# Memory attention with routed experts: one load of the gate weights, sums by two products, stores over two queues, a new order

## The chip, the cores and the metric

The kernel runs on one core of a Trainium2 chip. The metric is device time in microseconds (us), median of the timed runs. Engines are called PE (TensorE; PEld are its weight loads), DVE (VectorE), ACT (ScalarE), POOL (GpSimd) and SP (SyncE, which here issues loads and stores).

## What is computed

The reference has two parts. Attention over 32 memories for each of 8 batches and 8 heads (576 rows, 64 columns), then a mixture of 8 experts in which each of the 4608 rows goes to one expert.

```python
a = softmax(phi)                                  # 8 x 8 x 576 x 32, sums with 1e-9
k_m, v_m = a^T k, a^T v                           # per head: 32 memories x 64
attn = softmax(q k_m^T / 8)                       # 576 x 32
x = (attn v_m), heads side by side                # 4608 x 512
expert = argmax(x w_gate); gate = its probability # w_gate 512 x 8
out[row] = gate * relu(x w1[expert]) w2[expert]   # w1 512 x 1024, w2 1024 x 512
```

## The kernel before

Each batch b (0 to 7) is assumed to go to one expert: its guess is the most frequent expert of the batch (for batch 0 a guess from sums of the values). Rows that belong elsewhere ("strays") are listed in DRAM and done in slots of 64 rows at the end; of the last batch's rows, those that a stray slot wrote are added back from a DRAM buffer `late`. [...]

A batch has two parts. `front` makes the weights of the memories (steps A to C), the memory step E, which multiplies them with k and v (kvm), their sums D and scaling F, transposed keys G and G1, scores J, softmax K to M3 in a transposed layout, the high and low halves S and T of the attention weights, logits R, and the expert index by rank products X3, histogram R4 and index R6. LW loads w1 of that expert (four quarters), D0 to D3 load w2, W0 to W3 split it into halves. U0 and U1 multiply the memories' values with w1 (so that the experts' first layer works on 64 memories per head group), UH and UL split the result. `experts` makes the dense products: i00 to i17 (two halves of the rows, 8 column blocks, 6 products each), relu and split e, output products o (o00 to o33 in four row tiles of four parts with 6 products each, o40 to o43 for the tail of 64 rows with 4), evacuation y0 to y4, z for the tail, and stores.

The work of all engines follows one list, ORDER, written out by hand: "3X4" is step X4 of batch 3, "30J" step 0J (head group 0) of batch 3. `plan` calls the steps in that order, and each engine (PE, DVE, ACT, POOL, SP) keeps the order of its own instructions, so that a step waits for whatever stands ahead of it on its engine. Constants made before the list are free to move. Buffers: PSUM tag "mm" has 4 that are used in turn (pu of U0 and U1, ph, py), w1 and w2 share 6 raw buffers, output tiles y have 2, so that y of one tile waits until the stores of the tile two before have landed. At the start the PE does products on ones (`keep_warm`).

Lines that matter below: w_gate is loaded by three small loads on POOL's queue, twice in one layout (L172, for both halves of the partitions) and once in another (L173), copied in `constants_late` (L185). The sums of the memories' weights come in E, at the end, by products with `sel` (L304), a 64x32 tile for each head and half:

```python
for c in range(C + 1):
    ...
    nc.tensor.matmul(kvm[s][o0:o0 + 32, 2 * D:], lhsT=sel[s0, :], rhs=zp[s0, g, j:j + 1], start=True, stop=True)
```

and D adds 1e-9 (L310, two instructions) and takes the reciprocal (L311). `store` (L682) issues a tile's stores of 32 rows on SP; for the last tail of the last batch on ACT.

Of the kernel before, what the change touches and what calls it, by code (L numbers as in the profile page):

```python
# [27 lines left out]
0i11 0W1 0e15 0e10 1E 0i14 1D 0W2 10F 10Q 11Q 2L0 11F 0i13 0R3 1V 1V1 10G 0X 11G 1V2 0e14 1V3 1G1 0e11 0o00 0W3 10J
0X3 10K1 10K 0o01 0R4 0CE 0e13 10K2 10K3 11J 11K 0i16 11K1 0o10 0X1 11K2 0e16 11K3 10L 10M 20A 0o02 0o30 11L 10M0 10M1
0o03 10M2 2L1 0o11 0X4 11M 11M0 20A1 11M1 10M3 11M2 2LQ 0y0 0o31 0i17 11M3 21A 1R 1R1 1S1 1R2 1R3 0o12 0e17 0o40 1X3  # L30
0o32 0o33 1R4 0o13 11N 1R6 1X 1LW 0y3 0o41 1X4 0o42 0y1 21A1 1S0 1D3 0o20 2A2 10N 0o21 20Q 1D1 0o43 0o22 0o23 21B 1T0
20B 0X2 0X5 21Q 20C 21C 1U0 0y4 0y2 1T1 1UH10 0z 1U1 0X6 1UL10 1UH01 1UH00 1UL01 2E 1UL00 1D0 1i00 1UH11 1i01 1i02 00N
# [35 lines left out]
7i13 7i07 7o00 7entries 7load21 7load13 7W2 7W3 7e04 7e13 7gather 7e07 7load20 7o01 7i11 7load10 7load11 7o02 7o03
# [15 lines left out]
def kernel(  # L84
# [16 lines left out]
    P = 128  # L101
# [546 lines left out]
    def experts(b, st):  # L648
# [30 lines left out]
        def row(i, t):  # L679
            return (4 * i + t) // (T // 2), (4 * i + t) % (T // 2)  # L680
# [461 lines left out]
```

## Time and profile before

| | us |
|---|---|
| median of 3 timed runs | 432.77 (432.46 to 433.3) |
| profiled execution, device time | 436.48 |
| its span, first to last instruction | 434.7 |
| PE busy | 418.5 |
| DVE, ACT, POOL busy | 270.5, 192.8, 190.2 |

The profile comes from one execution, whose own time is 436.48 us. Busy times of engines overlap; the ends of products are modelled, so that a PE that is called busy may still stand between two starts. The rows on which the prediction rests stand in a section of their own.

### The profile page before, as it was taken

Reading aid. Unit: us, or ns where it says so; the run is one execution under the profiler, and the core shown is the slowest. Engines: PE = TensorE matmul, PEld = TensorE weight load, DVE = VectorE, ACT = ScalarE, POOL = GpSimd, SP = SyncE. Lnnn points to the kernel's source line nnn. Section 1 sums busy time; section 2 is a strip of 40 time slices with the busy share of each in tenths; the row PEclk is TensorE's granted clock in tenths of the full one; section 3 lists DMA queues with packets and bytes.
Section 4 is the critical chain, followed back from the end, with each engine's and each line's share of the span. In section 5 each row is a group of like instructions: output and inputs, shape, how many; then the busy total and the mean of one; then the engine's idle time right before and its main releaser. Section 6 shows DMA issues by size and latency. Waiting matters only on the chain.

```text
span 434.7 us, 11303 instructions
## 1 busy us (share of the span) xinstructions
PE 418.5 (96%) x4339; PEld 327.3 (75%) x4339; DVE 270.5 (62%) x690; ACT 192.8 (44%) x515; POOL 190.2 (44%) x270
## 2 busy tenths in 40 slices
PE   8879999899999999999999999999999999999992
PEld 4539787578867888688877887778869877698871
DVE  5478777386654777467645767569646756546422
ACT  3158424463345624463526434554247521745610
POOL 4565641047135453167044442366305866663530
PEclk9999999999999999999999999999999999999997
DMA  8898885790697817593277825694186007776302
GB/s 256 311 398 328 285 336 181 244 344 8 168 331 231 314 53 237 171 362 142 77 271 255 307 78 147 230 341 157 58 279 199 2 27 240 205 249 196 100 19 60
DMA packets 46411, 89.12 MB, mean 205 GB/s; under 512 B 6878, under 2 KB 14350, under 8 KB 46352
## 3 DMA queue, kind: packets, MB, share of 16 engines
q1 hardware_dynamic: 43376, 83.40, 56.7%
q0 software_dynamic: 2880, 4.80, 3.2%
q8 instruction: 36, 0.59, 0.5%
q14 instruction: 23, 0.19, 0.1%
q10 hardware_dynamic: 96, 0.13, 0.1%
HBM read 71.29 MB, written 17.40 MB: 204 GB/s over the span
## 4 chain that ended last, share of the span: by engine, by line
PE 88%; DMA 6%; DVE 1%; SPq 1%; ACT 1%; issue 1%; ACTq 0%
PE py L708 39%; PE ph L674 25%; PE py L627 6%; PE sT L425 4%; PE pu L363 4%; DMA wraw<-in_moe_w_dram 4%; PE kvm L301 4%; DMA kv<-in_v_dram 2%; PE lg L468 1%; PE pk L322 1%; PE sph L627 1%; PE spy L627 1%; SPq L597 1%; DMA out_dram<-y 1%; PE pv L333 1%
## 5 line engine op out<-in xcount | busy, mean ns | idle before, releaser
L708 PE MATMUL py<-whi,hh 128*128 128x512 f32 x256 | 101.8, 398 | 0.0
L708 PE MATMUL py<-wlo,hh 128*128 128x512 f32 x256 | 100.1, 391 | 0.0
L708 PE MATMUL py<-whi,hl 128*128 128x512 f32 x256 | 99.7, 390 | 0.0
L592 POOL TENSOR_TENSOR wlo<-wraw,whi 128x1024 fp32r<-128x1024 f32 x25 | 60.4, 2422 | 76.7 <-ACT whi L591 67.5
L674 PE MATMUL ph<-eh,uh 128*128 128x288 f32 x256 | 78.5, 307 | 0.7 <-DVE ul L370 0.7
L618 DVE SCALAR_TENSOR_TENSOR hl<-ph,hh 128x224 fp32r<-128x224 f32 (+1 forms) x128 | 52.5, 418 | 41.4 <-ACT ht L615 21.3
L674 PE MATMUL ph<-el,uh 128*128 128x288 f32 x256 | 75.5, 295 | 0.4 <-POOL el L1019 0.4
L674 PE MATMUL ph<-eh,ul 128*128 128x288 f32 x256 | 75.6, 295 | 0.1
L615 ACT ACTIVATE hh<-ph 128x224 fp32r<-128x224 f32 (+1 forms) x128 | 48.0, 385 | 44.8 <-PE ph L674 41.2
L708 PEld LDWEIGHTS py<-whi,hh 128*128 128x128 f32 x256 | 48.1, 188 | 12.5 <-issue 3.4
L708 PEld LDWEIGHTS py<-whi,hl 128*128 128x128 f32 x256 | 48.1, 188 | 10.5
L674 PEld LDWEIGHTS ph<-eh,uh 128*128 128x128 f32 x256 | 48.0, 188 | 9.9 <-issue 5.5
L708 PEld LDWEIGHTS py<-wlo,hh 128*128 128x128 f32 x256 | 48.1, 188 | 8.7
L583 POOL DMA_INDIRECT stray_list<-pay,posi x40 | 43.1, 1078 | 21.3 <-issue 10.2
L674 PEld LDWEIGHTS ph<-eh,ul 128*128 128x128 f32 x256 | 48.1, 188 | 1.1 <-DVE ul L370 0.3
L674 PEld LDWEIGHTS ph<-el,uh 128*128 128x128 f32 x256 | 48.1, 188 | 0.8 <-POOL el L1019 0.8
L721 ACT ACTIVATE y<-py,gw 128x512 f32<-128x512 f32 x31 | 21.3, 688 | 53.0 <-PE py L708 29.6
L591 ACT CAST whi<-wraw 128x1024 fp32r<-128x1024 f32 x33 | 34.5, 1052 | 0.4 <-DMA wraw<-in_moe_w_dram 0.4
L370 DVE TENSOR_TENSOR ul<-pu,uh 128x512 fp32r<-128x512 f32 x32 | 21.1, 680 | 21.0 <-ACT uh L367 17.1
L526 POOL COPY gw<-gw 64x1 f32<-64x1 f32 x8 | 1.9, 236 | 55.7 <-DVE gw L520 55.7
L627 PE MATMUL py<-whi,ht 128*128 128x512 f32 x64 | 25.2, 394 | 0.0
L363 PE MATMUL pu<-wraw,vT 64*32 64x512 f32 x256 | 21.7, 601 | 3.2 <-DMA wraw<-in_moe_w_dram 1.5
(211 smaller groups left out, 635.5 us busy)
## 6 DMA issues: line engine op xcount, KB each, us to landing
wraw<-in_moe_w_dram SPq DMA_DIRECT2D x72, 512.0 KB
kv<-in_v_dram SPq DMA_DIRECT2D x16, 576.0 KB
kv<-in_k_dram SPq DMA_DIRECT2D x16, 576.0 KB
qt<-in_q_dram SPq DMA_DIRECT2D x16, 576.0 KB
out_dram<-y SPq DMA_DIRECT2D x142, 64.0 KB
pt<-in_phi_dram SPq DMA_DIRECT2D x16, 288.0 KB
ad<-s_t POOLq DMA_DIRECT2D x15, 288.0 KB
stray_list<-empty SPq DMA_DIRECT2D x5, 336.0 KB
```

The source lines that it names most:

```text
L301: nc.tensor.matmul(kvm[s][o0:o0 + 32, 0:2 * D], lhsT=as_[g][s0, j, c, :], rhs=kvs[g][s0, :, j, c, :], start=(c == 0), stop=(c == C - 1))
L363: nc.tensor.matmul(pu[s, n0][32 * c:32 * c + 32, :], lhsT=vT[s0, b % 2, c, :], rhs=raws[c][s0, n0:n0 + DM], start=True, stop=True)
L370: nc.vector.tensor_tensor(out=ul[:, g, n0:n0 + DM], in0=pu[g, n0], in1=uh[:, g, n0:n0 + DM].bitcast(F32), op=ALU.subtract)
L583: nc.gpsimd.indirect_dma_start(out=ld_list[i][:, :], out_offset=bass.IndirectOffsetOnAxis(ap=posi[:, i:i + 1], axis=0), in_=pay[:, i, :], ...
L591: nc.scalar.copy(out=hi, in_=raw)
L592: eng.tensor_tensor(out=lo, in0=raw, in1=hi.bitcast(F32), op=ALU.subtract)
L615: nc.scalar.activation(out=hi, in_=ph, func=AF.Relu)
L618: nc.vector.scalar_tensor_tensor(out=lo, in0=ph, scalar=0.0, in1=hi.bitcast(F32), op0=ALU.max, op1=ALU.subtract)
L627: nc.tensor.matmul(o, lhsT=l, rhs=r, start=start, stop=stop)
L674: nc.tensor.matmul(ph, lhsT=lhs[:, g, fs], rhs=rhs[:, g, s0:s1], start=(n == 0), stop=(n == 5))
L708: nc.tensor.matmul(py, lhsT=lhs[:, f, i * P:i * P + P], rhs=rhs[:, f % 2, :], start=(f == 0 and n == 0), stop=(f == KF - 1 and n == 2))
L721: nc.scalar.activation(out=y, in_=v["py", i], func=AF.Copy, scale=gate)
```

## The change

Four edits. w_gate is loaded once (64 partitions) and copied to the other half on POOL; the third tile `wg` goes, and `wgs` is filled from `wgh`. The sums of the memories' weights come from two products per batch (one for each half s) with a `sel` that is repeated four times, so that every row of kvm gets the sums of all four (group, head) columns; a mask `quarter` with a one for the own quarter picks the right one. The last batch's tiles with `late` rows store half of their rows from ACT's queue. ORDER is a new list with the same steps.

```diff
-    sel = const.tile([P, M], F32, name="sel")
+    sel = const.tile([P, 4, M], F32, name="sel")
+    quarter = const.tile([P, 4], F32, name="quarter")
...
-        for j in range(2):
-            nc.gpsimd.dma_start(out=wgh[64 * j:64 * j + 64], in_=w_gate.rearrange("(h d) e -> d h e", d=D))
-        nc.gpsimd.dma_start(out=wg, in_=w_gate.rearrange("(c p) e -> p c e", p=P))
+        nc.gpsimd.dma_start(out=wgh[0:64], in_=w_gate.rearrange("(h d) e -> d h e", d=D))
...
-        nc.vector.tensor_reduce(out=sel, in_=ident.rearrange("p (c m) -> p m c", c=4), axis=AX.X, op=ALU.add)
+        nc.gpsimd.tensor_copy(out=wgh[64:128], in_=wgh[0:64])
+        nc.vector.tensor_reduce(out=quarter, in_=ident.rearrange("p (c m) -> p c m", c=4), axis=AX.X, op=ALU.add)
+        nc.vector.tensor_reduce(out=sel[:, 0], in_=ident.rearrange("p (c m) -> p m c", c=4), axis=AX.X, op=ALU.add)
+        nc.vector.tensor_copy(out=sel[:, 1:4], in_=sel[:, 0:1].broadcast_to([P, 3, M]))
...
-            nc.gpsimd.tensor_copy(out=wgs[s0, :, h, :], in_=wg[s0])
+            nc.gpsimd.tensor_copy(out=wgs[s0, :, h, :], in_=wgh.rearrange("p (c h) e -> p c h e", h=2)[s0, :, h, :])
...
-        kvm = [ps_at.tile([P, 2 * D + 1], F32, name="kvm", tag="at") for s in range(2)]
-        for c in range(C + 1):
+        kvm = [ps_at.tile([P, 2 * D + 4], F32, name="kvm", tag="at") for s in range(2)]
+        for c in range(C):
...
-                            nc.tensor.matmul(kvm[s][o0:o0 + 32, 2 * D:], lhsT=sel[s0, :], rhs=zp[s0, g, j:j + 1], start=True, stop=True)
+        for s in range(2):
+            s0 = slice(64 * s, 64 * s + 64)
+            nc.tensor.matmul(kvm[s][:, 2 * D:], lhsT=sel[s0].rearrange("p c m -> p (c m)"), rhs=zp[s0].rearrange("p g j -> p (g j)"),
+                             start=True, stop=True)
...
+        own = sm.tile([P, 2, 4], F32, name="zown")
         rz = sm.tile([P, 2], F32, name="rz")
         for s in range(2):
-            nc.vector.tensor_scalar(out=rz[:, s:s + 1], in0=kvm[s][:, 2 * D:], scalar1=1e-9, scalar2=None, op0=ALU.add)
+            nc.vector.scalar_tensor_tensor(out=own[:, s], in0=kvm[s][:, 2 * D:], scalar=1e-9, in1=quarter, op0=ALU.add, op1=ALU.mult)
+        nc.vector.tensor_reduce(out=rz, in_=own, axis=AX.X, op=ALU.add)
...
-        def store(i, y, n, eng=nc.sync):
+        def store(i, y, n):
...
+                eng = nc.scalar if ("late", i) in v and t >= n // 2 else nc.sync
...
-            store(i, y, TAIL // 32, nc.scalar if b == B - 1 else nc.sync)
+            store(i, y, TAIL // 32)
```

Of ORDER, the stretches that the prediction speaks of (batch 0 from scores to the first dense products; batches 1, 2, 3, 5 and 7 from the rank products to the first dense products; the last steps), before and after:

```diff
-00J 00K 0D0 00K1 0D1 0CL 00K2 01J 0V1 00K2b 00K3 01K 00K3b 01K1 0U0 00L 00Lb 01K2 01K2b 0U1 00M 0UH00 00Mb 01K3 1L1 01K3b 00M0 00M1 01L 0UH01 00M0b 10A 00M1b 0V2 0UH10 00M2 01M 00M2b 01M0 00M3 01M1 01Lb 0S0 01M2 0UL00 0T0 01Mb 01M3 0UH11 0D3 0S1 00M3b 0UL10 1LQ 0T1 01M0b 0S0b 0UL01 0V3 01M1b 0i00
+00J 00K 00K2 0V 0V1 00K1 00K2b 00K3 00K3b 00L 01J 01K 01K2 0U0 00M 00Lb 00Mb 00M0 00M0b 0UH10 01K3 00M1 01K1 0V2 1L0 00M1b 00M2 1L1 01K2b 01L 01M 0UH00 01M0 00M3 0UL00 01M1 0D2 0U1 10A 0S0 01K3b 01Lb 00M2b 0UL10 01M2 0UH01 01M3 01Mb 0S1 0T0 01M0b 0UH11 0T1 0D0 0UL01 01M1b 0UL11 00M3b 0V3 0D1 11A 1LQ 01M2b 0i00
...
-1X3 0o32 0o33 1R4 0o13 11N 1R6 1X 1LW 0y3 0o41 1X4 0o42 0y1 21A1 1S0 1D3 0o20 2A2 10N 0o21 20Q 1D1 0o43 0o22 0o23 21B 1T0 20B 0X2 0X5 21Q 20C 21C 1U0 0y4 0y2 1T1 1UH10 0z 1U1 0X6 1UL10 1UH01 1UH00 1UL01 2E 1UL00 1D0 1i00
+1X3 0o40 1R4 1X 1R6 0o13 21A 0o41 0X5 1X4 21Q 20Q 20A1 1LW 1S1 0o42 21A1 0y1 2A2 0y3 0o20 0o21 0o22 1S0 0o43 1X1 1D1 21B 0o23 0X6 10N 20B 1U0 0Y2 0y4 21C 00N 20C 1UH10 1T1 1D0 0z 11N 2E 1UH00 1UL00 1T0 0y2 1UL10 1U1 2D 1UH01 1UL01 1i00
...
-2X3 2R4 1e14 2X 2S1 1o31 1o32 2R6 1o33 1o20 0Y1 2T1 2X1 30A1 1o40 1o21 2LW 31A1 1y3 1o22 1o23 3A2 1o41 2D0 31Q 2X2 2S0 31B 30B 2U0
+2X3 1i14 2X 1i15 1e12 2R4 1o31 2R6 21N 2LW 1e15 1o20 1e14 1o32 31A1 3A2 31B 2D0 1o33 1o21 2S1 31C 2X1 1y3 30B 2S0 2T1 2X2 2D1 1o22 30C 0Y0 1X5 2T0 1o40 1o23 1o41 2U0
...
-3U0 40C 2o22 3T1 3T0 2y4 3D2 2z 3UH10 3UH00 3UL00 2o23 4E 3X4 41Q 2y2 4D 41F 3UL10 3U1 30N 3UH01 40F 3i00
+3U0 3UH00 3U1 3X5 40G 3UH10 41G 3X6 1Y0 3UH11 3UL00 4G1 3UL10 4V 3UH01 1Y4 3UL11 3UL01 3i00
...
-5X3 4e17 4o32 5R4 5R6 5S1 51N 5X4 5X 4o33 61A1 5LW 4y3 60A1 6A2 5X1 4o20 4o40 4o41 60B 5T1 61B 3Y3 60C 5D1 5S0 4o42 4o43 4o21 4o22 4y4 61Q 4o23 4X5 5D0 5T0 4X6 4y2 60Q 5U0
+5X3 4e17 5R4 5R6 61B 4o33 4o40 4o41 5LW 4o42 61Q 4o20 61C 5X4 5X 4o43 4o21 4o22 4y3 5T1 60B 5S0 5D1 4o23 4y4 5U0
...
-7X3 6o41 6o03 7R4 6o12 7S0 7R6 70N 6Y4 6o22 6o23 7X 7LW 7X1 6Y0 7X2 7T1 7X4 7X5 6o13 6o42 6y0 6y1 6o30 7X7 7X6 6o31 6o43 7D1 6y2 6y4 7table 7Y4 7U0 6o32
+7X3 6o03 7R4 6o22 7R6 7X4 7S0 6o12 6o40 5Y4 6o41 7LW 6o42 7X2 6X6 7T0 6Y1 6o13 6y0 7X5 6y1 6o23 6Y0 5Y2 6o43 7U0 7D1 6Y4 7table 6y2 7X6 6o30 6y4
...
-7finish 7o30 7late3 7o31 7scatter 7o32 7o33 7o40 7o41 7o42 7late4 7y3 7o43 7y4 7z
+7finish 7o30 7o31 7o32 7late4 7o33 7o40 7o41 7late3 7o42 7scatter 7y3 7o43 7y4 7z
```

## Rows read from the trace of the kernel before

**Rows 1.** The page, parts 1 and 2: busy us and share; granted PE clock.
```profile
PE 418.5 (96%) x4339; PEld 327.3 (75%) x4339; DVE 270.5 (62%) x690; ACT 192.8 (44%) x515; POOL 190.2 (44%) x270
...
PEclk9999999999999999999999999999999999999997
```

**Rows 2.** Windows: stretch, length, busy us (instructions) per engine, clock, DMA share, GB/s.
```profile
9.00:31.19 22.19, 18.31 (x331) 9.58 (x331) 13.41 (x32) 7.91 (x26) 12.63 (x42) 1.00 0.96 355
...
228.00:232.10 4.10, 3.27 (x169) 2.52 (x154) 2.28 (x5) 2.15 (x4) 1.24 (x2) 1.00 0.58 158
...
426.67:434.74 8.07, 0.00 (x0) 0.00 (x0) 2.23 (x3) 0.00 (x0) 0.00 (x0) 0.64 0.20 54
```

**Rows 3.** Chain of waits in order of time: start us, us, what.
```profile
16.87 7.84 DMA wraw<-in_moe_w_dram
...
31.19 5.92 PE ph L674 x43
...
70.01 7.89 DMA wraw<-in_moe_w_dram
77.91 3.11 DMA out_dram<-y
...
122.00 4.10 PE py L708 x18
126.11 0.93 PE py L627 x4
...
130.85 2.08 PE kvm L301 x138
```

**Rows 4.** DMA queues in the first 12 us; PE's first products in the timeline.
```profile
q0 software_dynamic: 96, 0.05, 7.1%
...
1.11 7.81 PE L229 MATMUL pw<-ones 128*128 128x448 f32 x14 [1.11 <-DVE ones L142]
```

**Rows 5.** Timeline at the start: start us, us, engine, line, operation, [idle before <- releaser].
```profile
25.83 0.58 ACT L367 CAST uh<-pu 128x512 fp32r<-128x512 f32 x1 [2.94 <-PE pu L363]
...
26.43 0.43 ACT L394 ACTIVATE s_t<-s_t 128x288 f32<-128x288 f32 x1
...
30.34 0.80 POOL L1019 TENSOR_TENSOR el<-eT,eh 128x288 fp32r<-128x288 f32 x1 [0.32 <-ACT eh L1015]
```

**Rows 6.** Timeline of weight loads in batch 0's memory step, merged runs.
```profile
15.29 0.32 PEld L304 LDWEIGHTS kvm<-zp,sel 64*32 64x32 f32 x16
15.62 0.30 PEld L229 LDWEIGHTS pw<-ones 128*128 128x128 f32 x2
```

**Rows 7.** Groups by line on DVE: busy us, mean ns of one, idle before.
```profile
L540 DVE SCALAR_TENSOR_TENSOR soh<-em,es,oh 128x40 f32<-128x40 f32 x8 | 2.0, 254 | 0.0
...
L310 DVE TENSOR_SCALAR rz<-kvm 128x1 f32<-128x1 f32 x16 | 1.7, 150 | 4.7 <-PE kvm L304 4.7
```

**Rows 8.** Timeline of PE and PEld: rank products and up-projections of batches 1, 2, 5, 7.
```profile
65.22 0.31 PE L548 MATMUL pr<-oh,tri 128*128 128x40 f32 x2
...
115.01 0.31 PE L548 MATMUL pr<-oh,tri 128*128 128x40 f32 x2
...
127.81 0.14 PEld L363 LDWEIGHTS pu<-wraw,vT 64*32 64x32 f32 x4 [0.68 <-DMA wraw<-in_moe_w_dram]
...
275.96 0.18 PEld L363 LDWEIGHTS pu<-wraw,vT 64*32 64x32 f32 x16 [0.35 <-PE py L708]
...
356.73 0.39 PE L548 MATMUL pr<-oh,tri 128*128 128x40 f32 x2
...
370.67 0.18 PEld L363 LDWEIGHTS pu<-wraw,vT 64*32 64x32 f32 x14 [0.91 <-issue]
```

**Rows 9.** Timeline of the end, by engine.
```profile
426.65 1.54 DVE L716 SCALAR_TENSOR_TENSOR y<-py,gz,yl 128x512 f32<-128x512 f32 x2 [7.63 <-PE py L627]
...
427.43 2.60 SPq L686 DMA_DIRECT2D out_dram<-y  x4
...
429.00 0.95 ACTq L686 DMA_DIRECT2D out_dram<-y  x2
```

More of the change, by code (lines that the diff above doesn't have):

```diff
@@ L28 @@
[L28 to L32, printed above, removed]
@@ L68 @@
[L68 to L72 removed]
+0L 00A 01A 01A1 00A1 0A2 00B 01B 0Z 01C 00C 0Z1 0Z2 0R6 0E 00Q 0D 00F 00G 01F 0LW 01G 01Q 0CL 0G1 00J 00K 00K2 0V 0V1
@@ new lines @@
+10K 11J 0W3 10K1 0X3 10K2 11K1 0e13 10K3 0R4 0X 0o02 0X1 11K 11K2 10L 10M 0o03 0e14 0e16 0o10 10M0 2L1 11K3 0X2 11L
+11M 0X4 11M0 0CY 0o11 10M1 11M1 11M2 0o30 10M2 10M3 11M3 0o31 0o32 0y0 0i17 1R 20A 0e17 1R1 1R2 1R3 0o33 0o12 1X3 0o40
+1R4 1X 1R6 0o13 21A 0o41 0X5 1X4 21Q 20Q 20A1 1LW 1S1 0o42 21A1 0y1 2A2 0y3 0o20 0o21 0o22 1S0 0o43 1X1 1D1 21B 0o23
+0X6 10N 20B 1U0 0Y2 0y4 21C 00N 20C 1UH10 1T1 1D0 0z 11N 2E 1UH00 1UL00 1T0 0y2 1UL10 1U1 2D 1UH01 1UL01 1i00 1i02
+1UH11 20F 1UL11 21F 1i03 21G 2V 20G 1e02 1i01 1e03 1e00 1D2 1W1 2G1 1i04 3L0 2V1 20J 1i16 1i05 1e01 1e04 20K 1W0 1i06
@@ new lines @@
+1e05 21J 1e06 1e16 2V2 1i13 20K1 20K2 1i07 1i11 20K3 21K 1o00 1o01 21K1 1e13 1o10 1D3 3LQ 21K2 1W2 1e07 1i10 1e11 1o11
+21K3 20L 1X2 3L1 20M 0Y1 1W3 21L 21M 20M0 1i17 1o02 20M1 1e10 1o03 21M0 21M1 21M2 20M2 20M3 30A 1y0 31A 1o12 21M3 2V3
+1o13 30A1 2R 2R1 1i12 20N 2R2 2R3 1y1 1e17 1o30 2X3 1i14 2X 1i15 1e12 2R4 1o31 2R6 21N 2LW 1e15 1o20 1e14 1o32 31A1
+3A2 31B 2D0 1o33 1o21 2S1 31C 2X1 1y3 30B 2S0 2T1 2X2 2D1 1o22 30C 0Y0 1X5 2T0 1o40 1o23 1o41 2U0 1y2 3E 2UH10 2UH00
+31Q 2UL00 1o42 2W0 1o43 3D 2UL10 2X4 4L1 31F 2i00 30F 3V 30G 1y4 3V1 1z 30Q 31G 2e00 3V2 3G1 2i01 2U1 2W1 2e01 30J
@@ new lines @@
+2UH01 2UH11 2UL01 2UL11 30K 2i02 2i13 2e02 2i06 2e13 2e06 2i03 2i05 30K1 2e03 2D3 2i12 2i14 2e05 2e12 2D2 4LQ 2e14
+2i10 4L0 2i07 2e10 30K2 2W2 2X5 30K3 2W3 2i04 2o00 2e07 2e04 41A 2i16 30L 31J 31K 31K1 2o01 2e16 31K2 30M 3V3 30M0
+31K3 2o02 2i11 0Y3 2e11 31L 30M1 0Y4 31M 2o10 2o03 30M2 2o11 2y0 2X6 31M0 2i17 31M1 31M2 30M3 2o12 1X6 40A 2i15 31M3
+2o13 3R 3S1 3R1 3R2 2e17 2o30 31N 3X 3R3 2y1 2Y4 2o31 41A1 2Y1 30N 2e15 3X3 3R4 2o32 2Y2 3S0 3R6 2o33 2o40 40A1 4A2
+2o41 40B 3LW 2y3 3D0 3X1 2o20 40C 2o42 41B 41C 3T0 3T1 2Y0 2o21 3X4 3X2 40Q 41Q 2o43 4E 3D3 2o22 2y4 4D 40F 2o23 2z
@@ new lines @@
+41F 2y2 3U0 3UH00 3U1 3X5 40G 3UH10 41G 3X6 1Y0 3UH11 3UL00 4G1 3UL10 4V 3UH01 1Y4 3UL11 3UL01 3i00 3D1 3D2 3e00 1Y2
+3i03 40J 40K 3i13 3i01 3i02 3e03 40K1 3W0 41J 3i05 3e13 3i07 40K2 41K1 3W1 5LQ 3W3 3e01 3e02 5L1 3e05 3i06 41K 3i04
+3e07 3i11 51A 41K2 3e06 41K3 3W2 3e04 3o00 3o01 40K3 3o10 41L 3o11 3e11 40L 41M 3o02 41M0 40M 3Y0 40M0 41M1 41M2 5L0
+3i15 2Y3 40M1 50A 3o12 3o13 3o03 4V1 3e15 50A1 3y1 3y0 4V2 3i10 40M2 41M3 3i16 4V3 51A1 3i14 40M3 3e10 3e16 3i12 3i17
+3e14 4R 4R1 40N 4R2 3e12 1Y3 3o30 4R3 3o31 4X3 3e17 4S0 3o32 4R4 5A2 3o33 4R6 3o40 4T0 4X 51B 4X4 51C 4X2 3o20 3o41
@@ new lines @@
+5R3 5X3 4e17 5R4 5R6 61B 4o33 4o40 4o41 5LW 4o42 61Q 4o20 61C 5X4 5X 4o43 4o21 4o22 4y3 5T1 60B 5S0 5D1 4o23 4y4 5U0
+60C 6E 60Q 4z 5D0 5UH10 5UL10 5UH00 4y2 5W1 5U1 5UL00 5T0 5UH01 5UH11 5i00 5i11 6D 4X6 5UL01 5i01 61F 5UL11 60F 5e00
+60G 61G 6V 5D3 4Y0 5e11 5i03 5i04 5W0 6G1 5e03 6V1 60J 5i14 60K 6V2 61J 5e01 5i07 5i02 5W3 5e04 5e14 61K1 5X1 5i10
+5i05 5X2 5e07 5D2 5e02 60K1 5i06 5e10 5o00 5i12 5e05 60K2 5o10 5o11 4Y2 5e06 5W2 5X5 61K 60K3 5o01 5o02 5o03 5i15 60L
+61K2 61K3 7L0 60M 70A 61L 7L1 5o12 5e12 6V3 60M0 60M1 3Y1 61M 61M0 5y0 60M2 61M1 60M3 70A1 5i13 5o13 61M2 5e13 5i17
@@ L142 @@
     nc.vector.memset(ones, 1.0)
-    wg = const.tile([P, KD, E], F32, name="wg")
     wgs = const.tile([P, KD, 2, E], F32, name="wgs")
```

74 lines of the change are left out of this document (26 added, 48 removed).

## Prediction, made before the change was run

> **What bounds the kernel now.** I read the page first: the span is 434.7 us, TensorE (PE) is busy 96% of it and its clock is granted in full in all slices but the last [rows 1]. So the PE's list of products sets the time, and a change can win only where the PE stands still, in the products it drops, or after the last product. The windows show where it stands still [rows 2]: 3.9 of the 22.2 us before dense work begins at 31.19; 0.8 of the 4.1 us around the memory step of batch 5; and all 8.1 us after the last product. Busy time hides more, because ends are modelled: the memory step of batch 5 fills a window of 4.1 us where the same step of batch 3 took 2.1 [rows 2, 3]. The chain of waits then tells what ends the stalls: the landing of the guessed expert's w1 at the start (16.87 + 7.84 = 24.71), the same landing in batch 1 (70.01 + 7.89 = 77.90), and there the row stores behind it (77.91 + 3.11 = 81.02) [rows 3]. The clock needs no term: it stays at its upper level until the products are over.
>
> The profiled execution took 436.48 us, with 434.74 between its first and last instruction; the median of the three timed runs is 432.77. I make the sum as a difference on the span and carry it to the median unchanged. A measurement of this kernel can tell about 0.2% (0.9 us) from no change.
>
> **w_gate once.** Two of three small loads go. In the first 12 us the software queue, which carried these three, took 7.1% of 16 engines [rows 4]: 0.85 us, so two thirds, 0.57 us, come off a stream that runs without a hole until q is in. What follows is paced: value sums, guess, expert index, then w1. The PE's warm-up products last until 8.9 [rows 4], when the values' sums begin, so not all of it is won: I take 0.4 of the 0.57 for w1's landing, 24.3. The copy on POOL replaces a wait on POOL; POOL's constants are due long after. Cost nothing; if it were late, the guess would be late by as much (it reads both halves of wgh), so 0 to +0.5.
>
> **The start in the new order.** Behind w1's landing (24.71) stands a queue on ACT [rows 3, 5]: 1.1 us later (25.83) it takes the first result of the up-projection (uh), 0.6 after that (26.43) the exponentials of the second head group; 4.7 later (30.34 + 0.80) that group's softmax has come to its last low half el, after steps with other steps between them on DVE, ACT and POOL, and the dense products begin at 31.19: 6.5 us after w1. In the new list 0UH10 stands ahead of 01L on ACT, so the exponentials wait behind one evacuation again, and 10A, UL00 and UL10 stand ahead of 01M3 as 10A and others did. So again 1.1 + 0.6 + 4.7, and only the earlier landing is left: **-0.3**. Bounds: -1.2, if the foreign steps are out of the chain because the first group's softmax now lies ahead of the uh; +0.8, if w1 lands no earlier and is slowed, since six loads of the next batch instead of three come right behind it.
>
> **The sums.** Per batch 16 products of a 64x32 stationary tile and one column go, and 4 of 64x128 and four columns come (fp32, so each product is two instructions). The 16 loads took 0.32 us from first start to last end, 14 ns apart; two 128-column loads took 0.30, so one starts 0.11 after the other [rows 6]. Removed: 16 x 14 = 0.22 us. Added: 4 x 0.11 = 0.44 if the two row halves take turns, 0.22 if they overlap as those of the 64x32 loads do. Over 8 batches 0 to +1.8; nearer the overlapping row, whose row halves are the same: **+0.5**. [...]
> DVE: two additions of 150 ns go; two fused operations (nearest row 254 ns, for 40 columns) and a reduction of that order come [rows 7]: at most +0.5 us between memory step and the scaled memories, taken +0.3. In batches 1 to 7 the list keeps at least 2.4 us of products between memory step and first keys; before, it kept 2.0 in batch 1 and the keys did not wait there, so it is hidden. Without that cover it is +0.3 each. In batch 0 nothing covers it, but there the PE waits for w1 afterwards (24.71).
>
> **The waits before each up-projection.** From the rank products (X3) to the up-projection (U0) the PE has so many whole output steps (4.10 / 3 = 1.37 us), tail steps of 0.93 and X3 itself, 0.4 [rows 3, 8]. w1 was there 12.7 us after X3 in batch 1 (65.22 to 77.90) and 12.8 in batch 2 (115.01 to 127.81) [rows 3, 8]; the last of its four quarters of the products needs the last quarter of w1, some 0.75 after its start by an even share of its 1 us.
> - Batch 1: 7 whole and 3 tail steps before (12.7), 5 and 4 now (10.9): w1's last quarter is awaited 1 us. But U1 was the gate before, with 2.9 us lost, since the stores of y1 and y3 land behind w1 (81.02) and y4 and y2 wait for their buffers; 2E now stands between U0 and U1, so U1 comes 14.3 after X3 instead of 13.8: **-0.45**.
> - Batch 2: two dense steps (0.8 each) more, 13.4 instead of 11.8; the wait at 127.81 (0.68) goes: **-0.75**.
> - Batch 3: U0, U1 and i00 now stand together with 2.0 us for uh, ul of both halves instead of 6: **+0.3** (0 to 0.6).
> - Batch 5: 12.3 becomes 10.9. Here I only know that w1 was in time, as 16 loads ran without a break at 275.96 [rows 8]; 0 to 0.9, **+0.2**, near the lower end since nothing in that row shows that it had just come.
> - Batch 7: 12.7 becomes 10.9. Before, U0 stood 0.91 for the buffer of y2 (370.67, 13.9 after X3) [rows 8]; now U0 is free, but step o30 behind it takes y2's buffer: 13.9 against 12.0, 2.0 lost instead of 1.2: **+0.8**.
> - Batches 4 and 6: alike or 1.4 us more cover: 0.
> Sum **+0.1**.
>
> **The memory step of batch 5.** Its extra 1.9 us ends in gaps that the trace gives to no wait. 24 fewer PE instructions per batch and another order may move it, remove it or set it elsewhere: half of it, **-0.9** (0 to -1.9).
>
> **The end.** SP issued four stores of the last tiles from 427.43 to 430.03, ACT two until 429.95 [rows 9]. Now each issues three, and the last is out when the last sum on DVE is (about 429.0): 0.5 less. y4's late rows are fetched ahead of y3's; y3 began on DVE at 426.65, at the end of the tail's products, though four tail steps of 0.93 [rows 3] stand behind its own: it waited some 3 us for its late rows. It is now at the rear of these six loads (+0.3), or all land sooner (-0.7): I take -0.2. Together **-0.7** (-1.3 to -0.1).
>
> Other moved steps (W splits on POOL, D loads, zero and list fills 0CY, 0CE on SP): the list keeps 1.4 us or more between each split and its products, and list fills now stand ahead of the load 0D3, whose split is due after all dense products of batch 0's first half. Cost nothing; without that cover up to 1 us at one place.
>
> Sum: -0.3 + 0.5 + 0.1 - 0.9 - 0.7 = -1.3. Span 433.4, **median 431.5**.
>
> **Rivals.**
> - *w1 late (slower).* Place: the wait for w1 in batches 0, 5, 7, where less work or a longer queue stands before it. It decides once w1 lands over 11.7 us after X3; batches 1 and 2 show 12.7. Price: start +0.8 instead of -0.3, batch 5 +1.0 instead of +0.2, batch 7 one more us, since store and o30 follow w1: +2.9. 432.77 - 1.3 + 2.9 = 434.4. For: two rows of 12.7; against: batch 5 had no wait at 12.3.
> - *Nothing left (same).* The sums cost their upper bound (+1.3 on my term) because four wide loads take turns. 432.8.
> - *All cover holds (faster still).* Start -1.2, gap of batch 5 gone (-1.9), end -1.3, rest as above: 432.77 - 3.8 = 429.0.
> - That the change does not do what it says I rule out: loads, products and queues are written out.
>
> **How the numbers follow.** Forecast 0.42, w1 late 0.2, nothing left 0.2, all cover holds 0.18. The forecast's own spread is about 1 us either way, so a quarter of it falls within 0.2%. Faster: 0.75 x 0.42 + 0.18 = 0.5; slower: 0.2 and a fifth of "nothing left": 0.24; same: 0.26. The range reaches from "all cover holds" to past "w1 late", as its three prices are bounds of single rows: 428.8 to 434.8.
>
> **What would show it.** Right: dense ph products from about 30.9; w1's landing near 24.3; no wait at U0 of batch 2; a wait for w1 in batch 1 with U1 sooner; o30 in batch 7 some 14 us after X3; no memory step over 2.4 us; last stores issued by 429.5 less what was won before. Wrong: a memory step of 2.4 us in every batch (sums dearer), PE waits for w1 over 1 us in batches 5 and 7, or a new stretch of unexplained gaps elsewhere.

## The result, and the profile after

The changed kernel was slower: 438.61 us (median of 6, 435.58 to 440.08) beside 433.56 us of the kernel before (6 runs, same timing), a ratio of 1.0107 (95% interval 1.0064 to 1.0150), which is +4.6 us where -1.3 was forecast. Timed once more as run e12 it came to 1.0046 (1.0010 to 1.0081), +2.0 us. So it is slower, by some 2 to 5 us, and the size is uncertain. Single executions of either kernel differ by 3 to 8 us. The two profiled executions differ by 3.1 us (439.56 and 436.48; spans 437.8 and 434.7), and what follows explains those 3.1.

The page of after (busy us and share, granted clock, the instruction queue q8), against [rows 1]:

```profile
PE 422.0 (96%) x4243; PEld 328.3 (75%) x4243; DVE 270.4 (62%) x700; ACT 192.6 (44%) x515; POOL 191.2 (44%) x269
...
PEclk9999999999999999999999999999999999999997
...
q8 instruction: 35, 0.57, 0.6%
```

96 products are gone and PE is busy for 3.5 us longer, at the same clock (mean granted 0.994, before 0.993). The windows of after that answer to [rows 2], and one of a memory step without any foreign wait (batch 3):

```profile
9.00:31.65 22.65, 19.77 (x319) 9.91 (x319) 13.94 (x34) 8.36 (x27) 12.09 (x41) 1.00 0.94 336
231.07:233.95 2.88, 2.88 (x163) 2.39 (x147) 1.96 (x4) 2.21 (x4) 0.00 (x0) 1.00 0.38 94
129.88:132.41 2.53, 2.53 (x157) 2.31 (x141) 0.69 (x1) 2.14 (x4) 0.06 (x1) 1.00 0.39 100
429.53:437.83 8.30, 0.00 (x1) 0.00 (x0) 2.25 (x3) 0.00 (x0) 0.00 (x0) 0.68 0.19 52
```

Dense work begins at 31.65 instead of 31.19; the memory step of batch 5 takes 2.9 us instead of 4.1, that of batch 3 takes 2.5 instead of 2.2; the time behind the last product is 8.3 instead of 8.1. The chain of waits of after:

```profile
17.72 7.21 DMA wraw<-in_moe_w_dram
...
31.65 5.99 PE ph L679 x43
...
72.23 7.33 DMA wraw<-in_moe_w_dram
79.58 5.04 DMA out_dram<-y
...
188.55 8.80 DMA pt<-in_phi_dram
```

w1 lands at 24.93 in batch 0 (24.71 before, [rows 3]). In batch 1 the row stores behind w1 land 5.0 us after it, where it was 3.1. The last line is a late load of the next batch's phi, for which output products waited 1.1 us; no other trace of this kernel or its relatives shows it.

The 3.1 us by place (time from a step's first product to the next step's, both traces): start +0.5; memory steps of batches 1 to 7 together +1.55 (19.31 against 17.76, the sums of the rows in the table below); up-projections and their neighbours 0.0 (batch 1 +0.4, batch 2 -0.95, batch 3 -0.2, batch 4 +0.9, batch 5 +0.2, batch 7 -0.3); that phi load +0.9; the end +0.2. One row needs care: in the new order the memory steps of batches 2 and 6 begin beside the last products of an up-projection. The row of batch 6 (+1.0) so holds some 0.7 us in which PE waited for w1 of batch 5, and the up-projections are nearer +0.7 than 0.0.

### The profile page after: what moved, and what is told of

It is laid out like the page before. It is cut to its first block, busy times and chain, and to the rows that moved or that the text cites. A ratio compares the mean times of both kernels' runs of the same rounds, so it can differ in the third digit from the quotient of the medians.

```text
span 437.8 us, 11112 instructions
## 1 busy us (share of the span) xinstructions
PE 422.0 (96%) x4243; PEld 328.3 (75%) x4243; DVE 270.4 (62%) x700; ACT 192.6 (44%) x515; POOL 191.2 (44%) x269
## 4 chain that ended last, share of the span: by engine, by line
PE 72%; DMA 18%; SPq 3%; DVE 2%; ACT 2%; issue 1%; POOL 1%; ACTq 0%; DVEq 0%; POOLq 0%
PE py L714 32%; PE ph L679 21%; DMA ag<-ad,hidx 8%; PE py L632 4%; DMA wraw<-in_moe_w_dram 3%; PE pu L368 3%; PE kvm L301 3%; PE sT L430 3%; DMA out_dram<-y 2%; DMA pt<-in_phi_dram 2%; DMA kv<-in_v_dram 2%; PE lg L473 1%; SPq L602 1%; PE pk L327 1%; DMA yl<-late 1%
## 5 line engine op out<-in xcount | busy, mean ns | idle before, releaser
L679 PE MATMUL ph<-el,uh 128*128 128x288 f32 x256 | 75.6, 295 | 1.4 <-POOL el L1025 1.4
L623 DVE SCALAR_TENSOR_TENSOR hl<-ph,hh 128x288 fp32r<-128x288 f32 (+1 forms) x128 | 51.3, 415 | 39.7 <-ACT ht L620 23.2
L620 ACT ACTIVATE hh<-ph 128x288 fp32r<-128x288 f32 (+1 forms) x128 | 47.3, 384 | 43.7 <-PE ph L679 42.7
L727 ACT ACTIVATE y<-py,gw 128x512 f32<-128x512 f32 x31 | 21.1, 684 | 42.2 <-PE py L714 25.2
L375 DVE TENSOR_TENSOR ul<-pu,uh 128x512 fp32r<-128x512 f32 x32 | 21.0, 683 | 22.9 <-ACT uh L372 22.5
L368 PE MATMUL pu<-wraw,vT 64*32 64x512 f32 x256 | 23.4, 601 | 2.0 <-issue 1.3
```

The costliest lines, as they stand in the source:

```text
L368: nc.tensor.matmul(pu[s, n0][32 * c:32 * c + 32, :], lhsT=vT[s0, b % 2, c, :], rhs=raws[c][s0, n0:n0 + DM], start=True, stop=True)
L375: nc.vector.tensor_tensor(out=ul[:, g, n0:n0 + DM], in0=pu[g, n0], in1=uh[:, g, n0:n0 + DM].bitcast(F32), op=ALU.subtract)
L620: nc.scalar.activation(out=hi, in_=ph, func=AF.Relu)
L623: nc.vector.scalar_tensor_tensor(out=lo, in0=ph, scalar=0.0, in1=hi.bitcast(F32), op0=ALU.max, op1=ALU.subtract)
L679: nc.tensor.matmul(ph, lhsT=lhs[:, g, fs], rhs=rhs[:, g, s0:s1], start=(n == 0), stop=(n == 5))
L727: nc.scalar.activation(out=y, in_=v["py", i], func=AF.Copy, scale=gate)
```

## Experiments

Each ratio is to the kernel before, timed beside it, with its 95% interval.

### Which of the edits: e1 to e4

The edits of the diff ahead of the prediction are taken apart, with no line of their own: sums by two products alone (e1), new order alone (e2), all edits in the old order (e3), all but the sums (e4).

> The kernel before with the sums by two products alone, old order, old loads and stores. Theory A (the wide products cost more than I took: memory steps of 2.50 to 2.62 us in the changed kernel against 2.12 to 2.32 in the kernel before, about 0.3 each in 8 batches): +2.0 to +2.6 us, and the memory step of every batch at or above 2.45 us. Theory B (the sums cost the 0.5 us of the prediction and everything else is the order): +0 to +0.8 us.

> The kernel before with the new order alone: three loads of w_gate, 16 products for the sums, old stores. Theory A: the order costs what the sums don't explain, +2 to +3 us, with the second up-projection of batch 1 waiting for row stores as in the changed kernel (U1 at 82.9, loss over 2.5 us). Theory B: +4 to +5 us. If the order is harmless by itself (0 +- 1), the loss comes from the sums and from what they do to the order.

> The changed kernel with the order of before put back. Theory A: +1.5 to +2.6 us against before (sums +2.4, one load of w_gate -0.3, stores of the last tiles -0.5). Theory B: -0.8 to +0.3.

> The changed kernel with the sums by 16 narrow products as before. Theory A: 2.4 us faster than the changed kernel (438.6), so +2 to +3 against before. Theory B: within 0.8 us of the changed kernel, so +3.5 to +5 against before.

Measured: e1 1.0091 (1.0061 to 1.0120); e2 1.0220 (1.0182 to 1.0258); e3 1.0044 (1.0025 to 1.0063); e4 1.0139 (1.0109 to 1.0169). So the sums alone cost 4.0 us, the order alone 9.6, and both together with the other edits 4.6 or (e12) 2.0, far less than the two added. Neither theory has room for that: A was right on e1's sign and on e3, but the sums cost more than 2.4 alone and nothing in the new order. The lengths of the memory steps (us, batches 1 to 7) show why:

```
            1     2     3     4     5     6     7
before     2.24  2.66  2.21  2.12  4.07  2.14  2.32
after      2.50  3.16  2.52  2.50  2.87  3.14  2.62
e1         2.50  4.91  2.50  2.50  4.63  2.52  2.60
e2         2.21  2.86  3.37  3.90  2.59  2.75  2.32
e3         2.50  4.86  2.50  2.50  3.85  2.52  2.60
e4         2.21  3.00  3.44  4.45  2.59  2.75  2.45
e6         3.75  2.61  2.24  2.21  2.59  2.47  2.32
e7         2.50  3.43  2.50  2.31  3.74  2.31  2.50
e13        2.25  2.66  2.25  2.12  2.29  2.45  2.32
```

Two things lie in it. First, each step with the new sums is 0.26 to 0.38 us longer (batches 1, 3, 4, 7 of before and after, or e1). Second, single steps stand for 1 to 2 us, and which ones changes with the kernel. e1's step in batch 2 and e4's in batch 4, timeline of weight loads:

```profile
80.16 2.31 PEld L303 LDWEIGHTS kvm<-kv,pt 64*32 64x32 f32 x133 [0.27 <-issue]
84.43 0.17 PEld L303 LDWEIGHTS kvm<-kv,pt 64*32 64x32 f32 x10 [1.97 <-issue]
```

```profile
178.58 1.97 PEld L299 LDWEIGHTS kvm<-kv,pt 64*32 64x32 f32 x143 [0.37 <-DVE qT L957]
182.78 0.10 PEld L299 LDWEIGHTS kvm<-kv,pt 64*32 64x32 f32 x1 [2.23 <-issue]
```

PE stands for 1.97 and 2.23 us behind 134 products of the step (one stands ahead of the row's 133) and behind 143, and waits for nothing that is shown. In all six such stalls of e1 to e4 there are 128 to 143 products ahead, and counted in order of time from the first PE instruction the places lie 1012 to 1014 matmul and load instructions apart: 1964 and 1966 (e1, e3), 2978 (e2, e4) and 3990 (e2, e4). Beside each the queue that the page calls q8 instruction moves a packet of 16 KB; at 35 or 36 packets in the span that is one for some 240 of PE's 8500 matmul and load instructions, from which I take them for PE's. DMA queues of e4 from 180.3 to 181.4 (packets, MB, share):

```profile
q8 instruction: 1, 0.02, 5.6%
```

### Does the stall follow the count of instructions: e6

The same kernel as e4, with 84 more PE instructions in front of all others and the same work:

```diff
-    keep_warm(7, ps_mm, "mm", 448)
+    keep_warm(28, ps_mm, "mm", 112)
```

> The new order with one load of w_gate, new stores and the old sums (run e4), and only the products on ones at the start cut in four: 56 of 112 columns instead of 14 of 448, so the same work and 84 more PE instructions in front of all others. Theory F (the memory steps of batches 3 and 4 stand because the next 16 KB of PE instructions arrive late when a whole piece lies in narrow products; e2 and e4 stood at product 127 or 128 of the step in batch 3 and 141 or 142 in batch 4): the piece boundaries move 42 products earlier, to about 85 and 99, where the slow steps ahead of the memory step give the fetch time; stalls there fall from 1.2 and 1.7 to 2.2 us to under 0.5 each, and the time by 2 to 4 us against e4 (442.0). Rival G (the stall belongs to the place, a memory step straight behind an up-projection, whatever the count): both stalls stay, time within 1 us of e4.

Measured: the memory steps of batches 3 and 4 (weight loads, both below) run through, and batch 1 and batch 0 stall instead, behind 132 and 134 products:

```profile
131.55 1.96 PEld L299 LDWEIGHTS kvm<-kv,pt 64*32 64x32 f32 x135 [0.28 <-issue]
...
177.66 1.98 PEld L299 LDWEIGHTS kvm<-kv,pt 64*32 64x32 f32 x144 [0.37 <-DVE qT L957]
...
43.34 1.89 PEld L299 LDWEIGHTS kvm<-kv,pt 64*32 64x32 f32 x132 [0.16 <-DVE lmx L477]
46.68 0.15 PEld L299 LDWEIGHTS kvm<-kv,pt 64*32 64x32 f32 x9 [1.46 <-issue]
```

By count these are instructions 1204 and 444, that is 760 apart and again 760 ahead of 1964. All distances are multiples of 253 to within two, near the some 240 to a packet of q8. So the stalls go by the count of PE's instructions, as theory F has it, and G falls: at such a place (a boundary, below) PE stands 1.2 to 2.2 us where the 128 products or more ahead of it are all narrow ones of one memory step (14 ns each, 1.8 us for 128). In the traces of these eight stalls PE goes on 2.3 to 2.7 us after the packet beside the stall begins to move. That its next instructions come late is F's reading of these numbers; no trace shows what PE waits for. The time, 1.0106 (1.0053 to 1.0159), is 1.4 us below e4, less than the 2 to 4 expected, and the intervals overlap. Of the two stalls that came, the one in batch 0 stands ahead of a wait for w1, and the one in batch 1 lies at a boundary where e4 already stood, 12 wide products behind the step (its instruction 1201):

```profile
45.97 0.19 PEld L707 LDWEIGHTS py<-wlo,hh 128*128 128x128 f32 x1 [1.87 <-issue]
```

So a stall can also fall just behind a memory step. Why the time fell no further is not settled.

The changed kernel meets such a boundary too. Between the first and the second product of U1 in batch 1, right behind a memory step, 1.9, 0.8, 1.4 and 1.6 us pass from start to start in after, e8, e11 and e12. By count this is instruction 1963, the boundary of the stalls of e1 and e3. In after, PE's products:

```profile
82.89 0.61 PE L368 MATMUL pu<-wraw,vT 64*32 64x512 f32 x1
84.81 1.74 PE L368 MATMUL pu<-wraw,vT 64*32 64x512 f32 x15 [1.31 <-issue]
```

The third of them starts at 85.47, once the row stores have landed and ACT has emptied a buffer behind them. So the stores still end this wait, and in this trace earlier stores could win 0.66 us of it, not the whole.

### The sums at the other end of the step: e7

e1 with the two products ahead of the 144 narrow ones instead of behind:

```diff
+        for s in range(2):
+            nc.tensor.matmul(kvm[s][:, 2 * D:], ...)
         for c in range(C):
...
-        for s in range(2):
-            nc.tensor.matmul(kvm[s][:, 2 * D:], ...)
```

> The kernel before with the two-product sums alone (run e1), but the sums ahead of the 144 narrow products of the memory step instead of behind. Theory H (the wide loads must wait until the narrow 64x32 products are through, 0.20 us of idle ahead of them in every batch): the 0.2 us stays, only at the other end, or goes where the step before is of 128 rows; memory step 2.3 to 2.5. Rival (each wide load costs 0.1 wherever it stands): 2.5 in every batch. Either way 0 to 1.6 us less than e1, and the stall of 2.0 us in batch 2 of e1 moves or goes, since the 144 products come 4 products later.

Measured 1.0045 (1.0015 to 1.0075), 2.0 us below e1 (the intervals overlap), by the traces most of it because the stall of batch 2 shrank from 1.97 to 0.86. The step of batch 3, weight loads, in after (sums last) and in e7 (sums first):

```profile
129.88 2.00 PEld L301 LDWEIGHTS kvm<-kv,pt 64*32 64x32 f32 x136 [0.28 <-issue]
132.09 0.30 PEld L306 LDWEIGHTS kvm<-zp,sel 64*128 64x128 f32 x4 [0.20 <-issue]
```

```profile
129.23 0.30 PEld L300 LDWEIGHTS kvm<-zp,sel 64*128 64x128 f32 x4 [0.36 <-ACT uh L374]
129.55 1.98 PEld L307 LDWEIGHTS kvm<-kv,pt 64*32 64x32 f32 x144
131.72 0.19 PEld L681 LDWEIGHTS ph<-eh,uh 128*128 128x128 f32 x1 [0.20 <-issue]
```

The four wide loads take 0.30 wherever they stand (the rival), and the 0.20 of idle stands where the narrow 128-column products end and wide tiles follow (theory H). With the old sums that idle is not there: their 16 loads run while those products end, and the next wide load starts 0.02 us behind them. The same step in before:

```profile
132.66 0.31 PEld L304 LDWEIGHTS kvm<-zp,sel 64*32 64x32 f32 x16
132.99 0.19 PEld L674 LDWEIGHTS ph<-eh,uh 128*128 128x128 f32 x1
```

So the 16 narrow loads were nearly free, 0.22 of loads in place of 0.20 of idle, and the four wide ones are 0.3 on top. Where narrow tiles follow (batches 4 and 6 in e7) the step takes 2.31, 0.2 above before. Both theories had a part.

### Places of the order: e8, e11, e12

Moves in the order of the changed kernel; the first two are e8, all four e11, none e12:

```diff
-1U0 0Y2 0y4 21C 00N 20C 1UH10 1T1 1D0 0z 11N 2E
+1U0 0Y2 0y4 21C 20C 1UH10 1T1 1D0 0z 2E
...
-1i00 1i02
+1i00 1i02 00N 11N
...
-7o32 7late4 7o33 7o40 7o41 7late3 7o42
+7o32 7late3 7late4 7o33 7o40 7o41 7o42
...
-4X3 3e17 4S0 3o32 4R4 5A2 3o33 4R6 3o40
+4X3 4R4 4R6 3e17 4S0 3o32 5A2 3o33 3o40
...
-7e03 7D3 7W0 7i10 7e01 7D2 7i05 7e10 7i07
+7e03 7D3 7i10 7e01 7D2 7i05 7e10 7i07 7W0
```

> The changed kernel with two places of the order altered. First, the writes of attention weights 00N and 11N (288 KB each, on the software queue) of batch 1 stand behind the first dense products instead of between w1's load and the second up-projection. Theory J (they share the DMA engines with the row stores that U1 of batch 1 waits for: the last of these landed 5.0 us behind w1, in the kernel before 3.1): the stall at U1 of batch 1 falls from 2.7 to 1.5 us or less. Rival (stores land late because they are issued late, as earlier ones free their slots): it stays at 2.5 or more. Second, the late rows of y3 are fetched ahead of those of y4, as before: y3's late rows land 0.3 to 0.6 us earlier and the end after the last product is 7.5 to 8.0 us instead of 8.3. Together 1 to 2 us less than the changed kernel (438.6, ratio 1.0107).

> The changed kernel with four places of its order altered: late rows of y3 first, 00N and 11N later (both as in e8), the steps 4R4 and 4R6 directly behind the rank products of batch 4 (there w1 was asked for 3.18 us after them instead of 2.47 in the old order), and the weight split 7W0 behind the products 7i07 (in four of five traces of the new order dense products of batch 7 waited 1 to 1.5 us for evacuations behind splits on ACT). If the order's cost lies in these places: 3 to 4 us less than the changed kernel, ratio 1.000 to 1.004 against before, with what is left the sums (2.4 us). If they only shift the waits: 1.005 or more.

> The changed kernel itself, once more, beside e11 on the same chip. Expected: the ratio of 1.0107 (1.0064 to 1.015) again; its trace tells which of its waits recur: U1 of batch 1 (2.7 us), the first dense products of batch 3's output (0.9, a softmax behind a late load), U1 of batch 4 (0.6 to 1.4), and no stall of over 0.4 us inside memory steps beyond the 0.3 of the sums.

Measured: e8 1.0054 (1.0021 to 1.0087), e11 0.9985 (0.9953 to 1.0017), e12 1.0046 (1.0010 to 1.0081). Timed together e11 is 2.6 us below the changed kernel, near the 3 to 4 expected. Of e8's two theories J is not tested. The stores of batch 1 still land 4.4 us behind w1 and U1 loses 2.1 us, but three writes of 288 KB still go out there, at 74.6, 76.6 and 77.2 us against 75.6, 77.6 and 78.1 in after: a list position orders a step only among steps of its own engine, and POOL runs ahead of the list when it has nothing to wait for. What makes these stores late stays open. The second edit is right: with the late rows of y3 first, DVE starts on y3 9.06 us after the first product of 7o30 instead of 9.71, and the end comes after 7.4 us instead of 8.3. In e12 the stalls of batches 1 and 4 recur (2.2 and 0.8 us with neighbours; 1.6 of the 2.2 at the boundary shown above), the wait for phi in batch 3 does not. In e11 batch 4 loses 0.4 instead of 0.8; what batch 7's dense products lose hardly moved (2.0 against 2.4), so the split 7W0 is not shown to be its cause.

### The memory step of batch 5: e5, e14, e9, e10, e13, e15

Before, this step lost 1.9 us. e5 and e14 are one kernel, before with one load of w_gate and the last stores over two queues; the others move steps in its order (old against new place):

```diff
 e9, e10
-4U1 3Y0 4UL00 4UH11 4UH01 5E 3Y1 4D1
+4U1 4UL00 4UH11 4UH01 5E 4D1
...
-4i00 50F 4UL11 1Y2
+4i00 3Y0 50F 4UL11 3Y1 1Y2
...
 e10 alone
-1i12 1i14 1e15 2R3 1o30 1e12 2X3 2R4
+1i12 1e15 2R3 1o30 1e12 2X3 1i14 2R4
```

> The kernel before with one load of w_gate and the last stores over two queues alone: old order, sums by 16 narrow products. Theory C (each of these two edits is a small gain, as predicted: about -0.3 at the start and -0.5 at the end): -0.5 to -1.5 us against before. Rival (they are worth nothing by themselves, the 2 us between sums alone and all edits in the old order come from other waits): within 0.5 us.

> Run e5 itself beside e13 on the same chip: 0.9978 (0.9947 to 1.0009) of the kernel before again, memory step of batch 5 at 3.5 to 4.2 us.

Measured 0.9978 (0.9947 to 1.0009) and 0.9955 (0.9933 to 0.9976): about -1.5 us, as theory C and the two terms of the prediction (-0.3, -0.5) have it, or a little more.

> The kernel before with one load of w_gate and the stores over two queues (run e5), and two list writes by index on POOL (3Y0, 3Y1) moved from beside the memory step of batch 5 to behind the first dense products of batch 4. Theory K (in six of six traces of the old order that memory step stands 0.1 to 0.2 us after such a write starts on POOL, for about 0.45 and 0.65 us, and in most once more at its end; in no trace of the new order does a write lie there): the step falls from about 4.1 to 2.1 or 2.2 us, and the time by 1.5 to 2 us against e5, to a ratio of 0.992 to 0.996 against before. Rival (the stall belongs to the PE's own instruction fetch, which runs there too): the step stays at 3.8 or more.

> Run e9, and one dense step of batch 1 (1i14) moved from ahead of the rank products of batch 2 to behind them, so that w1 of batch 2 is asked for 0.8 us of products earlier. If the wait of 0.5 to 1.1 us at the up-projection of batch 2 in the old order is for w1 alone: that wait falls by about 0.8 to under 0.3, time 0.4 to 0.8 us below e9. If row stores or buffers gate it as well: no change.

e9 0.9953 (0.9923 to 0.9984), e10 0.9978 (0.9951 to 1.0006). The step stayed at 3.5 and 3.9 us, but e9 did not test the theory: writes started there still, since the two that run beside the step are 1Y2 and 3Y2 (the 16th and 17th write on POOL), which stand later in the list. e14 shows one, with the loads of the step:

```profile
228.80 0.97 POOL L581 DMA_INDIRECT stray_list<-pay,posi  x1 [1.73 <-DMA stray_list<-pay,posi]
```

```profile
227.28 1.67 PEld L299 LDWEIGHTS kvm<-kv,pt 64*32 64x32 f32 x95 [0.25 <-issue]
229.38 0.14 PEld L299 LDWEIGHTS kvm<-kv,pt 64*32 64x32 f32 x2 [0.44 <-issue]
230.15 0.62 PEld L299 LDWEIGHTS kvm<-kv,pt 64*32 64x32 f32 x39 [0.63 <-issue]
```

The products stop at 228.94, 0.14 us after the write starts. e10's other edit brought nothing: its wait at the up-projection of batch 2 was 1.2 us in place of 0.4, so an earlier request for w1 alone does not end it; inconclusive beyond that.

e13 puts the right two writes behind a split that POOL waits for:

```diff
-4UL11 1Y2 4e00 4i01 4D2 4i06 4i16 3Y2 4e01 51F 50G 4W0 51G
+4UL11 4e00 4i01 4D2 4i06 4i16 4e01 51F 50G 4W0 1Y2 3Y2 51G
```

> Run e5 (one load of w_gate, stores over two queues, old order), and the two list writes by index that really lay beside the memory step of batch 5 (1Y2 and 3Y2; e9 moved two others, so writes still lay there) put behind the weight split 4W0 on POOL, which waits for its load until some 5 us after the memory step. Theory K (a write that starts on POOL stops the narrow products 0.10 to 0.16 us later for 0.45 and 0.65 us, in eight of eight traces of the old order): no write starts from 1 us ahead of the step to its end, no gap of over 0.3 us in it, and it takes 2.1 to 2.3 us instead of 3.5 to 4.1; time 1.3 to 1.9 us below e5. Rival (PE's instruction fetch, which runs there too, makes the gap): the step stays at 3.5 or more.

The step takes 2.29 us and has no gap of over 0.3 us, with 36 packets of q8 in the span as before. Theory K holds. Yet the time is 0.9981 (0.9957 to 1.0004), no better than e5. Its step of 135 loads at one go, and where the gain went:

```profile
226.46 2.01 PEld L299 LDWEIGHTS kvm<-kv,pt 64*32 64x32 f32 x135 [0.24 <-issue]
```

```profile
241.63 0.97 POOL L581 DMA_INDIRECT stray_list<-pay,posi  x1 [5.67 <-DMA stray_list<-pay,posi]
242.62 2.37 POOL L590 TENSOR_TENSOR wlo<-wraw,whi 128x1024 fp32r<-128x1024 f32 x1
...
245.04 0.19 PEld L707 LDWEIGHTS py<-wlo,hh 128*128 128x128 f32 x1 [1.15 <-POOL wlo L590]
```

3Y2 waits on POOL until 1Y2, a write to the same list, has landed; the split behind it is late, and output products wait 1.15 us here and 1.1 once more. e15 sets them apart:

```diff
-4W0 1Y2 3Y2 51G 5V 4e16 4i12 4i02 5G1 4W1
+4W0 51G 5V 4e16 4i12 4i02 5G1 4W1 1Y2
...
-50L 4W3 51K2
+50L 4W3 3Y2 51K2
```

> Run e13 with its two list writes apart: 1Y2 behind the weight split 4W1 and 3Y2 behind 4W3, so that the second no longer waits on POOL for the landing of the first ahead of 4W1 (in e13 POOL stood 5.7 us there and the first output products of batch 4 waited 2.4 us for that split). If that wait was what gave the gain back: memory step of batch 5 at 2.1 to 2.3 us as in e13, output steps of batch 4 without the waits, 1.2 to 1.9 us below e5 and e14 (0.9978 and 0.9955 of the kernel before), so 0.991 to 0.994. If the moved writes meet another wait: 0.995 to 0.998 again.

The output steps have no such wait, the memory step takes 2.65 (2.2, and 0.4 ahead of its third product), U1 of batch 4 now waits 1.1 us for an evacuation behind late stores, and the time is 0.9961 (0.9937 to 0.9986). This is faster than the kernel before and the changed one, but not measurably faster than e5 and e14: no run here turned the removed stall into time.

## Why the prediction was wrong, step by step

Between the forecast of -1.3 and the 3.1 us of the traces lie 4.4 us. The sums make 1.6 of them, the end 0.9, the late load of phi 0.9, the start 0.8, the up-projections 0.6 and the memory step of batch 2 another 0.2; that of batch 5 gives 0.6 back. The ratios (+4.6 us, and +2.0 in e12) are of medians, over executions that no trace shows.

- **The sums** are the term that was mis-sized: +0.5 was taken and 0 to +1.8 allowed; measured 0.3 us in each batch, 2.4 over eight (2.1 in batches 1 to 7; in batch 0 PE waits for w1 afterwards). The step that failed is "removed: 16 x 14 = 0.22 us". It priced the loads that go by their spacing in [rows 6] and did not ask what they cover: the 0.20 of idle at the change from narrow to wide tiles, which took their place. The price of what came was right: the four loads start as two pairs 0.11 apart, the two of a pair within 0.01, and take 0.30 in all, like the two 128-column loads of [rows 6], so their row halves overlap as the prediction took it. By themselves the added loads take what the removed ones took, 0.30 against 0.32; but the removed ones had covered the idle besides.
- **The stalls by count of instructions** were no term at all. They are worth 1.2 to 2.2 us for each boundary that falls on the end of a memory step: two steps in e2 and e4, one in e1 and e3, and none in after, where it falls on U1 of batch 1 and is covered by the wait for the stores. The two edits shift each other's boundaries, and so their costs do not add up. The prediction's "24 fewer PE instructions per batch and another order may move it, remove it or set it elsewhere" had the right words for the wrong stall.
- **The memory step of batch 5**: -0.9 was taken; from 4.07 to 2.87, of which +0.3 are sums, it is -1.5. The cause is not the count of PE's instructions but a list write on POOL, which the new order holds elsewhere (e13).
- **The start**: -0.3 was taken, +0.46 measured in the two traces. Over 17 traces w1 lands at 24.29 on average with three loads of w_gate (4 traces) and at 23.90 with one (13), -0.4 as the working said, but single executions lie between 22.9 and 25.2, so neither one trace nor these means can show it. "Again 1.1 + 0.6 + 4.7" failed by 0.23: from w1's landing to the dense products it is 6.48 to 6.57 in ten traces of the old order and 6.71 to 6.73 in seven of the new.
- **The up-projections**: +0.1 was taken, some +0.7 measured. Batch 2 (-0.75, measured -0.95) held. Batch 5 (+0.2) failed, at about +0.9 with the 0.7 that the list of places gives to the memory step of batch 6: U0 comes 11.1 us after X3, as the working had it (10.9), but w1's last quarter is there only 12.1 us after X3. In [rows 8] its loads ran without a break because U0 came 1.4 us later. In all seven traces of the new order PE waits for w1 there, 0.3 to 1.1 us. Batch 1 (-0.45) failed in "2E now stands between U0 and U1": the stores that gate U1 came 1.9 us later behind w1 than before, beside writes of 288 KB on the software queue that I had not followed and whose part in it no run shows. Batch 7 (+0.8) failed too, -0.3: w1 and the stores landed earlier after X3 (11.0 and 11.9 us, before 13.4 and 13.9), so o30 waited 1.61 us there, not 2.0, while U0 itself was free. Batch 4 was taken as unchanged and lost 0.9: w1 was asked for 3.18 us after the rank products, before 2.47, as 5A2, work of the next batch on DVE, stands between 4R4 and 4R6 in the list (e11, without it there, lost 0.4). The waits of after, weight loads of batches 1, 4, 5 and 7:

```profile
79.60 0.14 PEld L368 LDWEIGHTS pu<-wraw,vT 64*32 64x32 f32 x4 [0.76 <-DMA wraw<-in_moe_w_dram]
...
230.58 0.18 PEld L368 LDWEIGHTS pu<-wraw,vT 64*32 64x32 f32 x14 [0.88 <-ACT y L727]
...
279.23 0.14 PEld L368 LDWEIGHTS pu<-wraw,vT 64*32 64x32 f32 x4 [0.87 <-DMA wraw<-in_moe_w_dram]
...
371.97 0.19 PEld L714 LDWEIGHTS py<-whi,hh 128*128 128x128 f32 x1 [1.61 <-ACT y L727]
```

- **The end**: -0.7 was taken, +0.2 measured. The stores over two queues brought less than the 0.5 that was said: in the old order the span ends 17.37, 17.21 and 16.90 us after the first product of 7o30 with old stores (three traces), 16.0 to 17.0 with new ones (seven, mean 16.8), and in the new order e2 with the old stores and e4 and e6 with the new ones all end at 17.5. "-0.2" for the late rows had the wrong sign: fetched behind y4's, they let DVE begin at 429.95 in after, 0.4 us later against 7o30 than in [rows 9], and in the four other traces with the late rows in that order the span ends 17.0 to 17.5 us after 7o30, in the two of the new order with y3's rows first 16.7 and 16.8. After's end, DVE and the two queues:

```profile
429.95 1.54 DVE L722 SCALAR_TENSOR_TENSOR y<-py,gz,yl 128x512 f32<-128x512 f32 x2 [8.05 <-PEq L1116]
430.73 1.88 SPq L692 DMA_DIRECT2D out_dram<-y  x3
430.73 1.94 ACTq L692 DMA_DIRECT2D out_dram<-y  x3
```

- **The rivals**: none was the case as a whole. "w1 late" had the right sign, and in batch 5 its place and price as well (12.1 us after X3, +0.9 of the +1.0 said). In batch 7 and at the start it did not come (w1 11.0 us after X3; 24.93), and in batches 1 and 4 it was the stores behind w1 that came late. "Nothing left" named the sums' upper bound, and even that was 0.6 too low.

What stays open: e2's median lies 9 us above before while its one trace shows 5 (its profiled execution was the fastest of its runs), so some of the order's cost is in executions that no trace shows. In six of the new order's seven traces the dense products of batch 7 lose 1 to 2 us more than in the old; why is not settled.

## What to carry to other kernels

Small products that stand at a change of tile shape may be covering a pause that is paid anyway, here 0.20 us: before removing them, look at the idle ahead of the next instruction of the new shape. Where hundreds of short products follow each other, count instructions as well as time: here a stall of 1.2 to 2.2 us went by the count, and 84 instructions ahead of it moved it to other batches (e6). Two edits that change the count must be measured together (4.0 and 9.6 us alone, 4.6 or 2.0 together). And a list of steps orders each engine by itself: read from the trace where a step of an idle engine really runs before moving it.

## What the runs showed of the hardware that was not expected

- PE stood 1.2 to 2.2 us behind 128 to 143 products of 14 ns, with no wait shown, at places whose distances are multiples of 253 matmul and load instructions to within two (e1 to e4, e6), each beside a 16 KB packet of q8, and went on 2.3 to 2.7 us after that packet began to move; 84 more instructions at the start moved the stall to other batches. What PE waits for there was not shown.
- In the memory step of batch 5, a write by index that started on POOL stopped narrow products on PE 0.10 to 0.16 us later, for about 0.45 and 0.65 us, in eight traces of eight; with no write there (e13, e15, and the seven traces of the new order) these two gaps were gone. Through which part of the chip it acts was not tried.
- Narrow products (64x32 tiles, 128 columns) followed by wide tiles cost 0.20 us of idle between PE's weight loads (after and e7, batch 3); narrow products with one column between hid it (before, 0.02 us there).
